# Expert rows turned by VectorE from quarter-wise row loads, with smaller rooms for three experts

## The chip, the cores and the metric

The kernel runs on one core of a Trainium2 chip. A core has TensorE (PE; PEld is its loading of weights), VectorE (DVE), ScalarE (ACT), GpSimd (POOL) and SyncE (SP), which issues most DMAs. Each engine works through its own queue in order, and semaphores join the queues. The metric is the device time of one execution in microseconds (us); smaller is better. The kernel before takes 770.73 us (median of three runs, 770.66 to 772.34).

## What is computed

```python
def _attn_ref(r, k, v, w, u) -> np.ndarray:
    B, H, S, D = r.shape
    state = np.zeros((B, H, D, D), dtype=np.float32)
    y = np.zeros_like(r)
    for t in range(S):
        kt, vt, rt = (k[:, :, t], v[:, :, t], r[:, :, t])
        cur = np.einsum('bhd,bhe->bhde', u[None] * kt, vt)
        y[:, :, t] = np.einsum('bhd,bhde->bhe', rt, state + cur)
        state = w[None, :, :, None] * state + np.einsum('bhd,bhe->bhde', kt, vt)
    return y.astype(np.float32)

def _moe_ref(x, w_in, w_out) -> np.ndarray:
    h = x @ w_in
    g = h - np.tanh(h)
    return (g @ w_out).astype(np.float32)

def _moe2_ref(x, expert_emb, tau, w1, w2) -> np.ndarray:
    N, D = x.shape
    E = expert_emb.shape[0]
    xn = x / (np.linalg.norm(x, axis=-1, keepdims=True) + 1e-06)
    en = expert_emb / (np.linalg.norm(expert_emb, axis=-1, keepdims=True) + 1e-06)
    logits = xn @ en.T / tau
    expert_idx = np.argmax(logits, axis=1)
    logits_shift = logits - logits.max(-1, keepdims=True)
    probs = np.exp(logits_shift)
    probs /= probs.sum(-1, keepdims=True) + 1e-09
    gate_w = probs[np.arange(N), expert_idx]
    out = np.zeros((N, D), dtype=np.float32)
    for e in range(E):
        mask = expert_idx == e
        if not mask.any():
            continue
        h = np.maximum(x[mask] @ w1[e], 0.0)
        out[mask] = gate_w[mask, None] * (h @ w2[e])
    return out.astype(np.float32)

def reference(**kwargs):
    moe_kwargs = {k[4:]: kwargs[k] for k in kwargs if k.startswith('moe_')}
    moe2_kwargs = {k[5:]: kwargs[k] for k in kwargs if k.startswith('moe2_')}
    attn_kwargs = {k: kwargs[k] for k in kwargs if not k.startswith(('moe_', 'moe2_'))}
    attn_out = _attn_ref(**attn_kwargs)
    B, H, S, D = attn_out.shape
    x = np.ascontiguousarray(attn_out.transpose(0, 2, 1, 3)).reshape(B * S, H * D)
    x = _moe_ref(x=x, **moe_kwargs)
    return _moe2_ref(x=x, **moe2_kwargs)
```

There are 3072 tokens of 384 columns. An attention with decay (4 batches, 8 heads of 48) is followed by a feed-forward layer of 2048 columns with x - tanh(x), and by eight experts of 1024 columns with relu, of which each token takes the one with the largest logit. All is float32. The rows per expert are, for these inputs, 430, 401, 394, 382, 379, 373, 368 and 345.

## The kernel before

All large products are made of three matmuls: each operand x is split into a rounded half `hi` and a rest `lo` = x - `hi`, and hi*hi, hi*lo and lo*hi are summed in one PSUM bank. ScalarE copies the rounded half, VectorE or POOL subtracts.

**Tanh stage.** Tokens go in blocks of 384 (three tiles of 128), j = 0 to 7, over 16 chunks of 128 FFN columns. `ffn1` (line 557) makes `ph`, `small_tanh` makes `ghi` (line 625) and `glo` (line 635), and `ffn2` (line 572) adds to three banks `acc`, some steps later, so that PE has other products meanwhile. In the first two blocks the weights are converted in between: `split` (line 276) is a ScalarE copy (line 277) and a POOL subtraction (line 278), and `Logits.turn` turns two chunks of w_out on PE (line 293) and copies them out (`wt`, line 295), for the eight columns by which the logits come out of the same product.

**Routing.** `finish` finds the expert and the place of each row of a block. The row is copied from `acc` to `xr` (line 673), or for block 0 added to `part`, and POOL scatters it to `xe` in DRAM, where each expert has a region; `tab` gets 16 integers a row, with token and gate. The experts are sorted by their number of rows. For the expert of rank i there is room for 384 + `MORE[i]` rows (ranks 0 to 2) or 384 - `LESS[i]` (the others); what doesn't fit goes to a slower loop at the end, `overflow`.

**Expert stage.** `rows` (line 840) loads an expert's rows from `xe`, by one SP DMA for each tile of 128 (line 846), into `xg` (which lies in the tiles named `rkv`) or, for the overflow tile, `xo` (`ktab`, `u_bc`). `columns` (line 902) turns each tile by three PE transposes of 128x128 into the bank `pt` (line 908), from which ScalarE takes `hi` (line 910) and VectorE `lo` (line 912, columns `xt`, `x5`, `xn`). `wide` makes the FFN of 8 chunks: nine `ffn1` matmuls of the room's width, `relu` (`ghi` line 651, `glo` line 653), and `ffn2` two chunks later. Then `put` scales the rows by the gate (`ob`, line 917) and scatters them to the output. `narrow_half` does the first expert's overflow tile with tokens and columns exchanged: line 1036, then `half_b`, `ghi5` (line 1056) and `accn`.

`load_expert` brings an expert's weights in four quarters `eraw` (lines 859, 862), through two buffers in turn, so quarter c + 2 can be loaded when quarter c is converted (`wq`, ScalarE line 885, VectorE line 886; POOL does half of expert 0's). The rows of expert jb + 1 are asked for when expert jb begins, and are turned at its chunk 6. Only expert 1's rows can't be: the last block's rows are scattered while expert 0 is at work.

**Order.** A tile framework's scheduler decides in what order the instructions of one engine stand, by its own cost estimates; `tc.issue_after(x)` keeps what it encloses from being placed ahead of x. PSUM has eight banks, which all tiles of tag `p` share in turn.

Of the kernel before, what the change touches and what calls it, by code (L numbers as in the profile page):

```python
# [29 lines left out]
def rwkv__then__tanh_ffn__then__top1_moe_kernel(  # L30
# [36 lines left out]
    MORE = (64, 64, 32)  # L67
    KOV = len(MORE)
    LESS = (0,) * (E - 2) + (16, 32)
# [212 lines left out]
    class Logits:  # L282
# [5 lines left out]
        def turn(self):  # L288
            self.wts = []
            for i in range(2):  # L290
# [4 lines left out]
                nc.scalar.activation(out=wt, in_=pt, func=AF.Copy)  # L295
# [268 lines left out]
    def ffn2(i, span, g, rhs, acc, ts=None):  # L564
        for t in ts or range(len(acc)):
            m = acc[t].shape[0]
            if t == TB:
                parts = [(g[0][:, TOK:TOK + m], 0), (g[0][:, TOK:TOK + m // 2], 1)][::-1 if i == span[1] - 1 else 1]
            else:
                parts = [(g[a][:, t * P:t * P + m], b) for a, b in ((0, 0), (0, 1), (1, 0))]  # L570
# [69 lines left out]
    def relu(ph, n, i):  # L640
        m = n - TOK
        if m <= 0:
            ghi = work.tile([P, TOK], F32R, name="ghi", bufs=LAG + 1)[:, :n]
            glo = work.tile([P, TOK], F32R, name="glo", bufs=LAG + 1)[:, :n]
        elif i % 2 == 0:
            ghi = work.tile([P, n + m], F32R, name="ghi4", tag="am", bufs=4)
            glo = work.tile([P, TOK], F32R, name="glo4", tag="am", bufs=4)
        else:
            g = work.tile([P, n + m + TOK], F32R, name="g4", tag="tt")
            ghi, glo = g[:, :n + m], g[:, n + m:]  # L650
        a = nc.scalar.activation(out=ghi[:, :n], in_=ph, func=AF.Relu)  # L651
# [276 lines left out]
    def wide(jb, sl):  # L928
# [20 lines left out]
        for i in range(NE):  # L949
# [24 lines left out]
        for t, (gt, g) in enumerate(sl):  # L974
# [687 lines left out]
```

## Time and profile before

| | |
|---|---|
| median of three runs | 770.73 us (770.66 to 772.34) |
| the profiled execution | 771.22 us |
| its span in the trace | 769.6 us, mean granted clock 0.995 |
| PE busy | 756.2 us (98%), 6143 instructions |
| DVE busy | 464.8 us (60%), 1037 |
| ACT busy | 457.1 us (59%), 1064 |
| POOL busy | 300.5 us (39%), 362 |
| expert rows' DMAs on SP (page part 6) | 22 of 192 KB in the group `rkv<-xe`, 4.4 us to landing |

The profile page gives, for one execution, each engine's busy time, the same in 40 slices of the span, the DMA queues, the chain of work that ended last, and the costliest groups of instructions. In the slices PE is at nine tenths or more except for the first and the last one and one near the start, in which the granted clock was lower. The engines' shares are averages over stages: attention and weight conversion lie in the first 200 us, the tanh stage goes on to about 540, and the experts fill the rest.

### The profile page before, as it was taken

The numbers are of one execution on the slowest core, as the hardware profiler recorded it, in microseconds if no ns is written. First come the engines' busy times: TensorE is split into PE (matmuls) and PEld (weight loads), VectorE is DVE, ScalarE is ACT, GpSimd is POOL, SyncE is SP. The second block draws the span as 40 slices with busy tenths as digits, with TensorE's granted clock in tenths as the row PEclk, the third lists the DMA queues.
The fourth block names the chain that finished last, engine by engine and source line by source line (L and its number), as shares of the span: only waits on it lengthen the run. The fifth ranks groups of instructions, "written<-read, shape, count | busy, mean of one in ns | idle before, by whom it ended". The sixth has DMA issues, their size and how long they took to land.

```text
span 769.6 us, 15995 instructions
## 1 busy us (share of the span) xinstructions
PE 756.2 (98%) x6143; PEld 718.4 (93%) x6143; DVE 464.8 (60%) x1037; ACT 457.1 (59%) x1064; POOL 300.5 (39%) x362
## 2 busy tenths in 40 slices
PE   9899999999999999999999999999999999999996
PEld 5689899999999999999999999999989999999996
DVE  7967976667656565565555655656684455545430
ACT  5787676655657556656657756768463535544431
POOL 3743680466781671753564341133530202110111
PEclk9899999999999999999999999999999999999999
DMA  8964355243240330232223101052374435454400
GB/s 263 288 206 142 118 170 200 64 165 100 66 148 24 126 122 2 91 94 87 80 69 123 59 32 64 14 171 85 116 229 143 129 115 189 150 173 161 154 31 32
DMA packets 41016, 92.21 MB, mean 120 GB/s; under 512 B 4827, under 2 KB 20597, under 8 KB 39907
## 3 DMA queue, kind: packets, MB, share of 16 engines
q1 hardware_dynamic: 36274, 81.44, 33.0%
q0 software_dynamic: 4240, 9.67, 3.5%
q8 instruction: 50, 0.82, 0.4%
q14 instruction: 36, 0.29, 0.1%
q10 hardware_dynamic: 416, 0.00, 0.0%
HBM read 67.26 MB, written 24.00 MB: 119 GB/s over the span
## 4 chain that ended last, share of the span: by engine, by line
PE 90%; issue 3%; DVE 3%; ACT 2%; DMA 2%; POOL 1%; POOLq 0%; SPq 0%; DVEq 0%; ACTq 0%
PE acc L572 39%; PE ph L557 37%; PE py L454 5%; PE pa L423 3%; DMA eraw<-in_moe_w_dram 2%; PE pt L908 1%; PE warm L158 1%; PE pst L475 1%; POOL out_dram L827 0%; PE pt L293 0%; DVE bits L267 0%; DVE wraw L270 0%; PE pl L303 0%; DVE bits L264 0%; PE accn L1036 0%
## 5 line engine op out<-in xcount | busy, mean ns | idle before, releaser
L557 PE MATMUL ph<-xt,wq 128*128 128x384 f32 (+4 forms) x1712 | 340.1, 341 | 1.9 <-ACT wt L295 1.3
L557 PEld LDWEIGHTS ph<-xt,wq 128*128 128x128 f32 x1712 | 302.7, 188 | 5.9 <-ACT wt L295 1.5
L572 PE MATMUL acc<-wq,ghi 128*128 128x392 f32 (+2 forms) x1120 | 289.1, 343 | 0.9 <-ACT ghi L625 0.9
L572 PEld LDWEIGHTS acc<-wq,ghi 128*128 128x128 f32 (+1 forms) x1120 | 200.3, 187 | 5.9 <-ACT ghi L625 1.2
L572 PE MATMUL acc<-wq,glo 128*128 128x392 f32 (+2 forms) x552 | 182.2, 340 | 0.1
L612 ACT ACTIVATE z<-ph 128x384 f32<-128x384 f32 x128 | 62.8, 490 | 105.0 <-PE ph L557 104.7
L623 DVE TENSOR_TENSOR ph<-ph,z 128x384 f32<-128x384 f32 x128 | 72.0, 563 | 62.6 <-ACT z L612 62.0
L572 PEld LDWEIGHTS acc<-wq,glo 128*128 128x128 f32 (+1 forms) x552 | 102.7, 187 | 0.9 <-DVE glo L635 0.7
L635 DVE TENSOR_TENSOR glo<-ph,ghi 128x384 fp32r<-128x384 f32 x128 | 70.7, 553 | 45.7 <-ACT ghi L625 45.6
L827 POOL DMA_INDIRECT out_dram<-ob,gts x27 | 27.2, 1008 | 176.6 <-ACT ob L917 171.4
L625 ACT ACTIVATE ghi<-ph 128x384 fp32r<-128x384 f32 x128 | 62.6, 490 | 41.0 <-DVE ph L624 37.6
L615 ACT ACTIVATE q<-z,sb_t 128x384 f32<-128x384 f32 x128 | 78.9, 617 | 3.4
L624 DVE SCALAR_TENSOR_TENSOR ph<-q,ph 128x384 f32<-128x384 f32 x128 | 71.7, 560 | 12.5 <-ACT q L615 3.5
L629 ACT ACTIVATE mk<-z,lz_t 128x384 bf16<-128x384 f32 x128 | 77.1, 603 | 0.0
L653 DVE SCALAR_TENSOR_TENSOR glo<-ph,ghi 128x384 fp32r<-128x384 f32 (+2 forms) x56 | 30.7, 549 | 63.8 <-ACT ghi L651 63.8
L651 ACT ACTIVATE ghi<-ph 128x384 fp32r<-128x384 f32 (+4 forms) x56 | 27.5, 491 | 67.6 <-PE ph L557 67.5
L411 POOL TENSOR_TENSOR am<-ident,cd 128x512 f32<-128x512 f32 x36 | 36.8, 1045 | 77.8 <-DVE cd L397 77.1
L886 DVE TENSOR_TENSOR wq<-eraw,wq 128x768 fp32r<-128x768 f32 x60 | 55.1, 955 | 11.5 <-ACT wq L885 11.0
L885 ACT ACTIVATE wq<-eraw 128x768 fp32r<-128x768 f32 x64 | 50.4, 839 | 6.2 <-DMA eraw<-in_moe_w_dram 6.2
L278 POOL TENSOR_TENSOR wq<-wraw,wq 128x768 fp32r<-128x768 f32 (+1 forms) x17 | 30.3, 1782 | 39.6 <-ACT wq L277 38.5
L716 POOL DMA_INDIRECT tab<-tk,irow x24 | 24.4, 1019 | 31.8 <-DVE tk L744 25.1
L491 POOL TENSOR_TENSOR st<-st,pw 112x384 f32<-112x384 f32 x20 | 16.7, 840 | 49.2 <-DVE st L484 43.7
(287 smaller groups left out, 860.0 us busy)
## 6 DMA issues: line engine op xcount, KB each, us to landing
eraw<-in_moe_w_dram SPq DMA_DIRECT2D x32, 768.0 KB, 4.5
rkv<-in_rows_dram SPq DMA_DIRECT2D x18, 640.0 KB, 5.6
tt<-in_cols_dram SPq DMA_DIRECT2D x22, 448.0 KB, 4.4
xd<-xt SPq DMA_DIRECT2D x8, 1152.0 KB, 8.0
wraw<-in_moe_w_in_dram SPq DMA_DIRECT2D x8, 768.0 KB, 8.6
wraw<-in_moe_w_out_dram SPq DMA_DIRECT2D x8, 768.0 KB, 5.2
rkv<-xe SPq DMA_DIRECT2D x22, 192.0 KB, 4.4
xe<-zero SPq DMA_DIRECT2D x2, 1536.0 KB, 15.4
```

What stands on the lines that cost most here:

```text
L454: nc.tensor.matmul(out=self.py[32 * g:32 * g + 32, kk, :], lhsT=lhs, rhs=rhs, start=start, stop=stop)
L557: mark["ph"] = nc.tensor.matmul(out=ph, lhsT=lhs[a][:, kk, :], rhs=rhs(b, kk), start=(kk == 0 and p == 0), stop=(kk == nk - 1 and p == 2)).ins
L572: mm = nc.tensor.matmul(out=acc[t][:lhs.shape[1]], lhsT=lhs, rhs=rhs(b, i), start=(i == span[0] and p == 0), stop=(i == span[1] - 1 and p ...
L612: nc.scalar.activation(out=z, in_=ph, func=AF.Square)
L615: nc.scalar.activation(out=q, in_=z, func=AF.Square, scale=SS, bias=sb_t)
L623: nc.vector.tensor_tensor(out=ph, in0=ph, in1=z, op=ALU.mult)
L624: nc.vector.scalar_tensor_tensor(out=ph, in0=q, scalar=KC, in1=ph, op0=ALU.add, op1=ALU.mult)
L625: mark["ghi"] = nc.scalar.activation(out=ghi, in_=ph, func=AF.Copy).ins
L629: nc.scalar.activation(out=mk, in_=z, func=AF.Relu, bias=lz_t, accum_out=zx[:, step:step + 1])
L635: mark["glo"] = nc.vector.tensor_tensor(out=glo, in0=ph, in1=ghi.bitcast(F32), op=ALU.subtract).ins
L885: nc.scalar.activation(out=hi[c][:, a], in_=t[:, a], func=AF.Copy)
L886: engs[s % len(engs)].tensor_tensor(out=lo[c][:, a], in0=t[:, a], in1=hi[c][:, a].bitcast(F32), op=ALU.subtract)
```

## The change

1. Rows are stored with another order of columns (`by_quarter`, `quarters`): the 384 columns are seen as 3 x 4 x 32 (k, j, c) and written as (j, k, c). So a quarter j of a row, 96 columns in one piece of 384 bytes, holds for each k the j-th 32 columns of it.
2. `rows` loads a tile by four DMAs on SP instead of one: DMA j puts quarter j of all 128 rows on partitions 32 j to 32 j + 31, with the row's block of 32 and the 96 columns along the free axis.
3. `columns` then turns the whole tile by one VectorE instruction, which transposes blocks of 32x32, into the PSUM bank `pt`. What follows reads `pt` as before. (`plain` serves only the overflow loop.)
4. `MORE` goes from (64, 64, 32) to (64, 32, 16) and `LESS` from (0, 0, 0, 16, 32) for ranks 3 to 7 to (0, 0, 8, 16, 32). `relu`, `ffn2`, `joined` and `wide` pad the second half of an overflow tile to a multiple of 32 rows, and `order_rest` has four more small operations.
5. Two placements: the split of the chunk that comes just before the fifth pair of logit columns is held back until after that pair's `wt` copies, and the steps i = 13 and 15 of the last tanh block place expert 0's weight loads behind `ghi`, where before only i = 15 did.

```diff
-    MORE = (64, 64, 32)
+    MORE = (64, 32, 16)
     KOV = len(MORE)
-    LESS = (0,) * (E - 2) + (16, 32)
+    SQ = 32
+    NQ = P // SQ
+    DQ = DM // NQ
+    LESS = (0,) * (E - 3) + (8, 16, 32)
...
-                nc.scalar.activation(out=wt, in_=pt, func=AF.Copy)
+                mark["wt"] = nc.scalar.activation(out=wt, in_=pt, func=AF.Copy).ins
...
-                parts = [(g[0][:, TOK:TOK + m], 0), (g[0][:, TOK:TOK + m // 2], 1)][::-1 if i == span[1] - 1 else 1]
+                parts = [(g[0][:, TOK:TOK + m], 0), (g[0][:, TOK:TOK + (m + 31) // 64 * 32], 1)]
+                parts = parts[::-1 if i == span[1] - 1 else 1]
...
+        h = (m + 31) // 32 * 32
         if m <= 0:
             ghi = work.tile([P, TOK], F32R, name="ghi", bufs=LAG + 1)[:, :n]
             glo = work.tile([P, TOK], F32R, name="glo", bufs=LAG + 1)[:, :n]
         elif i % 2 == 0:
-            ghi = work.tile([P, n + m], F32R, name="ghi4", tag="am", bufs=4)
+            ghi = work.tile([P, TOK + 2 * h], F32R, name="ghi4", tag="am", bufs=4)
             glo = work.tile([P, TOK], F32R, name="glo4", tag="am", bufs=4)
         else:
-            g = work.tile([P, n + m + TOK], F32R, name="g4", tag="tt")
-            ghi, glo = g[:, :n + m], g[:, n + m:]
+            g = work.tile([P, 2 * TOK + 2 * h], F32R, name="g4", tag="tt")
+            ghi, glo = g[:, :TOK + 2 * h], g[:, TOK + 2 * h:]
...
+    def quarters(x):
+        return x.rearrange("p (k j c) -> p j k c", k=NK, j=NQ)
+
+    def by_quarter(x):
+        return x.rearrange("p (j k c) -> p j k c", k=NK, j=NQ)
...
-                nc.vector.tensor_tensor(out=x, in0=acc[t], in1=x, op=ALU.add)
+                nc.vector.tensor_tensor(out=by_quarter(x[:, :DM]), in0=quarters(acc[t][:, :DM]), in1=by_quarter(x[:, :DM]),
+                                        op=ALU.add)
+                nc.vector.tensor_tensor(out=x[:, DM:], in0=acc[t][:, DM:], in1=x[:, DM:], op=ALU.add)
...
-                nc.scalar.activation(out=xr, in_=acc[t][:, :DM], func=AF.Copy)
+                nc.scalar.activation(out=by_quarter(xr), in_=quarters(acc[t][:, :DM]), func=AF.Copy)
...
-            g = (xg[(jb % 2) * TB + t] if t < TB else xo[jb % 2])[:m]
-            mark["rows"] = nc.sync.dma_start(out=g[:, :DM], in_=xe[bass.ds(row + t * P, m), :]).ins
+            n = (m + SQ - 1) // SQ
+            g = (xg[(jb % 2) * TB + t] if t < TB else xo[jb % 2])[:, :n * DQ]
+            src = xe[bass.ds(row + t * P, n * SQ), :].rearrange("(i r) (j e) -> j r i e", r=SQ, j=NQ)
+            for j in range(NQ):
+                mark["rows"] = nc.sync.dma_start(out=g[j * SQ:(j + 1) * SQ].rearrange("r (i e) -> r i e", i=n),
+                                                 in_=src[j]).ins
...
-    def columns(sl, hi, lo, gate):
-
-        for t, (_, g) in enumerate(sl):
-            m = g.shape[0]
-            pt = ps.tile([P, NK, m], F32, tag="p", name="pt")
-            for kk in range(NK):
-                nc.tensor.transpose(pt[:, kk, :], g[:, kk * P:(kk + 1) * P], ident[:m, :m])
+    def columns(sl, hi, lo, gate, plain=False):
+
+        for t, (gt, g) in enumerate(sl):
+            m = gt.shape[0]
+            n = (m + SQ - 1) // SQ
+            pt = ps.tile([P, NK, n * SQ], F32, tag="p", name="pt")
+            if plain:
+                x = work.tile([P, DM], F32, name="xp", tag="z")
+                nc.scalar.activation(out=quarters(x), in_=by_quarter(g), func=AF.Copy)
+                for kk in range(NK):
+                    nc.tensor.transpose(pt[:, kk, :], x[:, kk * P:(kk + 1) * P], ident)
+            else:
+                nc.vector.transpose(out=pt.rearrange("p k (i r) -> p i k r", r=SQ),
+                                    in_=g.rearrange("p (i k c) -> p i k c", i=n, k=NK))
+            pt = pt[:, :, :m]
...
-                    nc.scalar.activation(out=part[:, t, :], in_=x, func=AF.Copy)
+                    nc.scalar.activation(out=by_quarter(part[:, t, :DM]), in_=quarters(x[:, :DM]), func=AF.Copy)
+                    nc.scalar.activation(out=part[:, t, DM:], in_=x[:, DM:], func=AF.Copy)
...
+            with tc.issue_after(mark["wt"]):
+                while held:
+                    split(*held.pop())
...
-            last = split(*ready[m])
+            if turns.get(i + 1) == 4:
+                held.append(ready[m])
+            else:
+                last = split(*ready[m])
...
-                with tc.issue_after(mark["ghi"]) if i == 15 else ExitStack():
+                with tc.issue_after(mark["ghi"]) if i >= 13 else ExitStack():
```

The scheduler makes of it other orders on several engines. On ScalarE, in the second block of the tanh stage, some 82 us into the trace, the rows were these before; `wt` are the turned columns of w_out, `wq_80` is a converted weight chunk:

```order
L615 ACTIVATE q<-z,sb_t 128x384
L629 ACTIVATE mk,zx<-z,lz_t 128x384
L312 ACTIVATE wq_79<-pw__1257 128x2x8
L277 ACTIVATE wq_80<-wraw 128x2x384
L295 ACTIVATE wt<-pt 128x384 x2
L625 ACTIVATE ghi<-ph 128x384
L612 ACTIVATE z<-ph 128x384
L615 ACTIVATE q<-z,sb_t 128x384
```

and are now these:

```order
L616 ACTIVATE z<-ph 128x384
L619 ACTIVATE q<-z,sb_t 128x384
L633 ACTIVATE mk,zx<-z,lz_t 128x384
L315 ACTIVATE wq_79<-pw__1255 128x2x8
L298 ACTIVATE wt<-pt 128x384 x2
L280 ACTIVATE wq_80<-wraw 128x2x384
L629 ACTIVATE ghi<-ph 128x384
L616 ACTIVATE z<-ph 128x384
L619 ACTIVATE q<-z,sb_t 128x384
```

The pair of `wt` copies has passed the weight chunk's copy.

On ScalarE in the last tanh block, around 512 us, `wq_72` and `wq_73` are the first two quarters of expert 0's weights, and `ex` and `se` belong to the gates of the block before. Before:

```order
L625 ACTIVATE ghi<-ph 128x384
L885 ACTIVATE wq_72<-eraw 128x768 x2
L612 ACTIVATE z<-ph 128x384
L615 ACTIVATE q<-z,sb_t 128x384
L629 ACTIVATE mk,zx<-z,lz_t 128x384
L885 ACTIVATE wq_73<-eraw 128x768 x2
L625 ACTIVATE ghi<-ph 128x384
L736 ACTIVATE ex<-l 128x24
```

and now:

```order
L633 ACTIVATE mk,zx<-z,lz_t 128x384
L629 ACTIVATE ghi<-ph 128x384
L752 ACTIVATE ex<-l 128x24
L616 ACTIVATE z<-ph 128x384
L755 ACTIVATE se<-se,half 128x3
L619 ACTIVATE q<-z,sb_t 128x384
L633 ACTIVATE mk,zx<-z,lz_t 128x384
L905 ACTIVATE wq_72<-eraw 128x768 x2
L629 ACTIVATE ghi<-ph 128x384
L905 ACTIVATE wq_73<-eraw 128x768 x2
L616 ACTIVATE z<-ph 128x384
```

The conversions stood in front of the `z` after which `ex` comes; now they stand behind `ex`, `se` and the operations of one more chunk.

On VectorE where expert 0 passes to expert 1, around 555 us, `glo_7287` and `glo_7314` before are `glo_7315` and `glo_7342` now (chunks 5 and 6 of expert 0); `wq30_81` and `wq31_82` are the first two quarters of expert 1's weights, `xt` and `x5` its columns, and lines 1091 to 1107 before (1120 to 1136 now) belong to a list of what overflows. Before:

```order
L653 SCALAR_TENSOR_TENSOR glo_7287<-ph_7276,ghi_7286 128x384
L886 TENSOR_TENSOR wq30_81<-eraw_7018,wq20_78 128x768 x2
L653 SCALAR_TENSOR_TENSOR glo_7314<-ph_7303,ghi_7313 128x384
L886 TENSOR_TENSOR wq31_82<-eraw_7020,wq21_79 128x768
L1091 TENSOR_TENSOR g1_7583<-jot_7566,exc_7581 128x168
L886 TENSOR_TENSOR wq31_82<-eraw_7020,wq21_79 128x768
L912 TENSOR_TENSOR xn_7330<-pt_7331,xn_7330 128x3x64
L1093 TENSOR_TENSOR sel_7584<-g1_7583,sel_7584 128x168
L912 TENSOR_TENSOR xt_7337<-pt_7339,xt_7337 128x2x128
L912 TENSOR_TENSOR x5_7338<-pt_7339,xt_7337 128x128
L1099 SCALAR_TENSOR_TENSOR exc_7581<-exc_7581,reg_144 128x8
L912 TENSOR_TENSOR xt_7337<-pt_7346,xt_7337 128x2x128
```

and now, from the transpose of the second tile on:

```order
L934 STREAM_TRANSPOSE pt_7370<-rkv1_124 128x4x3x32
L662 SCALAR_TENSOR_TENSOR glo_7315<-ph_7304,ghi_7314 128x384
L1126 TENSOR_REDUCE oex_7621<-g1_7613 128x21
L906 TENSOR_TENSOR wq30_81<-eraw_7027,wq20_78 128x768 x2
L1131 TENSOR_TENSOR g1_7613<-exc_7611,jp_7615 128x168
L1136 CAST ovi_151<-oex_7621 128x21
L934 STREAM_TRANSPOSE pt_7375<-rkv1_124 128x4x3x32
L940 TENSOR_TENSOR xt_7363<-pt_7370,xt_7363 128x2x128
L940 TENSOR_TENSOR x5_7364<-pt_7370,xt_7363 128x128
L662 SCALAR_TENSOR_TENSOR glo_7342<-ph_7331,ghi_7341 128x384
L934 STREAM_TRANSPOSE pt_7380<-u_bc_139 128x96
L1132 TENSOR_TENSOR g1_7613<-g1_7613,sel_7614 128x168
```

The transposes and joins of the columns have come in between the two `glo` and the conversions, and the conversion of `wq31_82` comes next after the last row shown. On PE the products from the second `glo` now stand behind the first products of the narrow tile, just ahead of expert 1's first `ffn1`.

## Rows read from the trace of the kernel before

**Rows 1.** Busy us by stretch (PE, PEld, DVE, ACT, POOL; clock; DMA; GB/s):

```profile
540.00:570.00 30.00, 30.00 (x178) 28.18 (x178) 22.39 (x82) 15.24 (x33) 14.21 (x23) 1.00 0.53 151
645.00:670.00 25.00, 25.00 (x147) 24.96 (x147) 12.10 (x19) 11.25 (x21) 2.96 (x3) 1.00 0.49 158
```

**Rows 2.** Groups of line 908: busy us, mean ns of one, idle before:

```profile
L908 PE MATMUL pt<-ident,rkv 128*128 128x128 f32 (+2 forms) x72 | 9.1, 271 | 0.0
```

**Rows 3.** Timeline, PE, expert 0's first tile: start us, us, instruction, count:

```profile
526.77 1.14 PE L908 MATMUL pt<-ident,rkv 128*128 128x128 f32 x9
527.67 0.60 PE L572 MATMUL acc<-wq,ghi 128*128 128x392 f32 x2
```

**Rows 4.** Groups by shape, line 557: busy us, mean ns, idle before:

```profile
L557 PE MATMUL ph<-xt,wq 128*128 128x448 f32 x64 | 15.9, 369 | 0.0
L557 PE MATMUL ph<-xt,wq 128*128 128x352 f32 x72 | 12.6, 323 | 0.0
```

**Rows 5.** Timeline, ACT and PE, 81 to 83; in brackets idle before:

```profile
81.41 0.88 ACT L277 ACTIVATE wq<-wraw 128x768 fp32r<-128x768 f32 x1
82.19 0.85 ACT L295 ACTIVATE wt<-pt 128x384 f32<-128x384 f32 x2
82.71 1.86 PE L557 MATMUL ph<-xt,wq 128*128 128x384 f32 x9 [1.33 <-ACT wt L295]
```

**Rows 6.** Timeline, ACT and PE, 506 to 522:

```profile
511.80 1.58 ACT L885 ACTIVATE wq<-eraw 128x768 fp32r<-128x768 f32 x2 [5.11 <-DMA eraw<-in_moe_w_dram]
521.51 0.98 PE L572 MATMUL acc<-wq,ghi 128*128 128x392 f32 x4 [0.91 <-ACT ghi L625]
```

**Rows 7.** Timeline, SP's DMA issues, expert 1's rows, then expert 2's:

```profile
547.80 0.57 SPq L846 DMA_DIRECT2D ktab<-xe  x1
548.59 2.35 SPq L846 DMA_DIRECT2D rkv<-xe  x3
586.44 1.52 SPq L846 DMA_DIRECT2D rkv<-xe  x3
```

**Rows 8.** Line 846 alone: issue ns min/median/max, first and last start:

```profile
L846 SPq DMA_DIRECT2D rkv<-xe x24: 332/345/904, 502.6 to 700.3; - x24
```

**Rows 9.** DMA issues, 545:560, then 560:568: KB, us to landing:

```profile
rkv<-xe SPq DMA_DIRECT2D x3, 192.0 KB, 2.9
tab<-tk,irow POOLq DMA_INDIRECT x3, 2.4
...
rkv<-xe SPq DMA_DIRECT2D x3, 192.0 KB, 6.3
```

**Rows 10.** Tile eraw, 490 to 600:

```profile
DMA to landing us min/median/max: 4.4/4.8/6.0
```

**Rows 11.** Timeline, DVE, 551 to 561:

```profile
551.12 0.56 DVE L653 SCALAR_TENSOR_TENSOR glo<-ph,ghi 128x384 fp32r<-128x384 f32 x1 [0.30 <-ACT ghi L651]
555.08 1.83 DVE L886 TENSOR_TENSOR wq<-eraw,wq 128x768 fp32r<-128x768 f32 x2 [0.18 <-ACT wq L885]
560.74 0.42 DVE L912 TENSOR_TENSOR xt<-pt,xt 128x256 fp32r<-128x256 f32 x1
```

**Rows 12.** Timeline, ACT and PE, 565 to 574:

```profile
565.63 3.04 ACT L885 ACTIVATE wq<-eraw 128x768 fp32r<-128x768 f32 x4
570.69 1.53 ACT L917 ACTIVATE ob<-acc,gts 128x384 f32<-128x384 f32 x3 [0.33 <-PE acc L572]
572.09 0.67 ACT L1056 ACTIVATE ghi<-pt 128x256 fp32r<-128x256 f32 x2
573.85 1.57 PE L1036 MATMUL accn<-wq,ghi 128*128 128x384 f32 x8
```

**Rows 13.** Busy us by stretch (as rows 1), then PE's timeline:

```profile
30.00:32.00 2.00, 0.43 (x2) 0.43 (x3) 2.00 (x5) 2.00 (x8) 1.89 (x2) 0.72 1.05 392
32.00:34.00 2.00, 1.14 (x6) 0.73 (x5) 2.00 (x3) 2.00 (x8) 2.00 (x2) 0.50 1.03 394
...
35.73 2.79 PE L557 MATMUL ph<-xt,wq 128*128 128x384 f32 x9
```

More of the change, by code (lines that the diff above doesn't have):

```diff
@@ L645, in relu @@
         elif i % 2 == 0:
-            ghi = work.tile([P, n + m], F32R, name="ghi4", tag="am", bufs=4)
+            ghi = work.tile([P, TOK + 2 * h], F32R, name="ghi4", tag="am", bufs=4)
             glo = work.tile([P, TOK], F32R, name="glo4", tag="am", bufs=4)
         else:
-            g = work.tile([P, n + m + TOK], F32R, name="g4", tag="tt")
-            ghi, glo = g[:, :n + m], g[:, n + m:]
+            g = work.tile([P, 2 * TOK + 2 * h], F32R, name="g4", tag="tt")
+            ghi, glo = g[:, :TOK + 2 * h], g[:, TOK + 2 * h:]
         a = nc.scalar.activation(out=ghi[:, :n], in_=ph, func=AF.Relu)
         for o, c in ((glo, slice(0, min(n, TOK))), (ghi[:, n:], slice(TOK, n)))[:1 + (m > 0)]:
-            v = nc.vector.scalar_tensor_tensor(out=o, in0=ph[:, c], scalar=0.0, in1=ghi[:, c].bitcast(F32),
-                                               op0=ALU.max, op1=ALU.subtract)
+            a0, a1 = ph[:, c], ghi[:, c].bitcast(F32)
+            if c.start and h > m:
+                o = o[:, :2 * h - m].rearrange("p (a b) -> p a b", b=m)
+                a0, a1 = (x[:, None, :].to_broadcast([P, (2 * h - m) // m, m]) for x in (a0, a1))
+            v = nc.vector.scalar_tensor_tensor(out=o, in0=a0, scalar=0.0, in1=a1, op0=ALU.max, op1=ALU.subtract)
         return (ghi, glo), {"a": a.ins, "v": v.ins}
+    def quarters(x):
+        return x.rearrange("p (k j c) -> p j k c", k=NK, j=NQ)
+    def by_quarter(x):
+        return x.rearrange("p (j k c) -> p j k c", k=NK, j=NQ)
     def finish(j, acc, part=None):
@@ L920, in joined @@
     def joined(acc):
-        m = acc.shape[0] // 2
+        h = (acc.shape[0] + 31) // 64 * 32
+        m = acc.shape[0] - h
         b = work.tile([P, DM], F32, name="half_b", tag="z")[:m]
-        nc.scalar.activation(out=b, in_=acc[m:], func=AF.Copy)
+        nc.scalar.activation(out=b, in_=acc[h:], func=AF.Copy)
         nc.vector.tensor_tensor(out=b, in0=acc[:m], in1=b, op=ALU.add)
@@ L958, in wide @@
             if len(pend) > lag:
-                acc.extend(ps.tile([P, DM], F32, tag="p", name=f"acc{t}")[:g.shape[0] * (1 + (t == TB))]
-                           for t, (_, g) in enumerate(sl) if i == lag)
+                acc.extend(ps.tile([P, DM], F32, tag="p", name=f"acc{t}")[:g.shape[0] + (t == TB and (g.shape[0] + 31) // 32 * 32)]
+                           for t, (g, _) in enumerate(sl) if i == lag)
                 ffn2(*pend.pop(0))
@@ L973, in wide @@
         prev = None
-        for t, (gt, g) in enumerate(sl):
+        for t, (gt, _) in enumerate(sl):
             with tc.issue_after(prev) if prev and jb == E - 1 else ExitStack():
@@ L985, in narrow @@
         xt = [work.tile([P, NK, P], F32R, name="xn", tag="q"), work.tile([P, NK, P], F32R, name="xn", tag="t", bufs=1)]
-        columns([slot], xt[0], ((xt[1], 0, NK),), {})
+        columns([slot], xt[0], ((xt[1], 0, NK),), {}, True)
         yield
@@ L1171, in general @@
                 nc.vector.tensor_copy(out=gt[:, 1:2].bitcast(F32), in_=g[:, DM:DM + 1])
-                for _ in narrow(0, (gt, g), alone=True):
+                for _ in narrow(0, (gt, g[:, :DM]), alone=True):
                     pass
@@ L1182, in gate_row @@
         junk = work.tile([P, DM], F32, name="gjunk", tag="t", bufs=1)
-        nc.scalar.activation(out=row[:, :DM], in_=acc[:, :DM], func=AF.Copy)
+        nc.scalar.activation(out=by_quarter(row[:, :DM]), in_=quarters(acc[:, :DM]), func=AF.Copy)
         nc.scalar.activation(out=junk, in_=row[:, :DM], func=AF.Square, accum_out=rn)
@@ L1446, in rwkv__then__tanh_ffn__then__top1_moe_kernel @@
     at = (-1, -1) + CONV
+    held = []
     turns = {at[order.index(2 * c + 1)] + 1: c for c in range(NF // 2)}
@@ L1610, in rwkv__then__tanh_ffn__then__top1_moe_kernel @@
             nc.gpsimd.dma_start(out=xo[0][:, :DM], in_=xe[bass.ds(row, P), :])
-            for _ in narrow(0, (gt, xo[0])):
+            for _ in narrow(0, (gt, xo[0][:, :DM])):
                 pass
```

## The prediction

> **What bounds the kernel now.** I read the page's first two parts first, then the busy times by stretch, then PE's waits, then the single instructions where the diff bites. TensorE is busy for all of 540 to 570 and of 645 to 670, at full clock, while VectorE has 22.39 of 30 and 12.10 of 25 us and ScalarE about half [rows 1]. So a PE instruction that goes away is time saved, and work given to VectorE costs nothing unless something that PE wants comes late. Outside the expert stage PE waits rarely; two of these waits lie where the change moves operations [rows 5, 6].
>
> **Removed: the transposes on PE.** Line 908 stands for 72 transposes of the full tiles [rows 2]; nine more, three each, turn the three overflow tiles: 81, nine for each of eight experts and nine for the overflow. Nine in a row are not worth their summed 1.14 us, since they overlap: the next product starts 0.90 us after the first of them [rows 3]. 9 groups x 0.90 = **8.1 us**, all of it on PE, where nothing else hides it.
>
> **Removed: columns of the first product.** FFN1 of an expert has 72 matmuls (8 chunks x 9). 448 columns take 369 ns and 352 take 323 [rows 4], so 46 ns for 96 columns. Rooms shrink by 32 (rank 1), 16 (rank 2) and 8 (rank 5): 56 x 72 x 46/96 ns = **1.9 us**. The narrower overflow products keep their column count, so they give nothing.
>
> **Moved: the held split.** At 82.71 PE had stood 1.33 us for the second of two `wt` copies on ScalarE, which stood behind a `wq` copy of 0.88 [rows 5]. In the new order (first pair of order fences) the copy stands behind them: the two come 0.78 earlier (82.19 - 81.41), and PE finds its columns that much sooner. Gain 0.8, and not the whole 1.33, since what is left is the two copies themselves. The subtraction that follows the copy is POOL's, and starts 0.8 later; it feeds a weight half that is read some steps on. Nothing else is queued on POOL that PE awaits there.
>
> **Moved: conversions of expert 0.** ScalarE stood 5.11 us for the first weight quarter, until 511.80, and what was behind it was late until PE stood 0.91 us for `ghi` at 521.51 [rows 6]. In the new order (second pair of fences) the first two conversions come two steps later, and the third about three. Against that, 9 more row loads stand ahead of the first weight load on SP: at 0.58 us each (below) it lands 5.2 later, at 517.0. ScalarE, which stood ready at 506.69 (511.80 - 5.11), gets there two steps of 3.2 and some 2.5 of their operations later, about 515.6; it stands 1.4, converts two halves (1.58), and `ghi` is out at 519.1, while PE wanted it at 521.51 - 0.91 = 520.6. The wait goes: gain **0.9**. At 0.80 a load `ghi` comes at 521.1 and half of it stays; the bounds are 0 and 0.9.
>
> Gains: 8.1 + 1.9 + 0.8 + 0.9 = **11.7 us**.
>
> **Added: the transposes on VectorE.** 27 instructions of up to 128x384. The trace has none. Every elementwise VectorE operation of that size takes 0.56 us [rows 11], and I take 0.55; twice that if it makes two passes, and not less. In the steady expert stretch VectorE is idle 12.9 of 25 us [rows 1], and a `glo` is used two steps after its `ph`, so 3 to 4 x 0.55 in each expert (25 us) is hidden: 0. On this price the Trainium skill ("VectorE: DVE Perf Modes", section "The three transpose paths") has 311 ns for a 128x128 bf16 tile, into SBUF, in 32x32 blocks. An estimate from it is 0.93 us for 384 columns; with three such instructions on the chain below the sum would be about 1 us higher, 764. No run of before shows the instruction.
>
> **Added: row loads.** 27 become 108. Where expert 1 follows expert 0 it cannot be hidden, since its rows become readable only at 547.80, when the last scatter is in. There 5 loads are issued, which land 2.9 us later [rows 7, 9]; now there are 20 on the same queue. The pace: three in 1.52 us in the steady state, the single one 0.345 [rows 7, 8], so (1.52 - 0.345)/2 = 0.58 us. At the boundary the first steps are slower: 548.59 - 547.80 = 0.79, and the slowest issue is 0.904. I take 1.0 for the first and 0.58 for the rest, and 2.9 to land: load 12 is there at 547.80 + 1.0 + 11 x 0.58 + 2.9 = 558.1, load 20 at 562.7.
>
> VectorE works in order, and the new order (third pair) puts the transposes ahead of `glo` and the weight conversions. From load 12 on: transpose 0.55 (558.65), `glo` 0.56, a conversion pair 1.83, a transpose 0.55, join 0.42 + 0.28, `glo` 0.56, a short transpose 0.3, the second pair 1.9, and four list operations between them 1.15 (an estimate, below the 0.42 for 256 columns): **566.2**. Only then is the buffer of the quarter free that the last weight load needs; that takes 4.8 (median [rows 10]): 571.0. ScalarE converts it (3.04 for four, 1.52 for two), and behind it in its queue stand three `ob` (1.53), a `ghi` (0.55) and the two `ghi5` (0.67) [rows 12]: 575.3; half of VectorE's work on these, 0.4: 575.7. PE's product from `ghi5` (`accn`) started at 573.85 [rows 12]; without the 1.6 us of transposes just ahead of it and 0.28 of columns it would at 571.97. **Cost 575.7 - 571.97 = 3.7 us**, seen as three waits: small for `glo`, about 1.3 for expert 1's columns, about 2.2 for `ghi5`.
>
> Bounds: at 0.50 us per load 0.9 less, 2.8. At the 0.80 of the boundary's first step load 20 decides: its chain ends at 548.8 + 19 p + 2.9 + 0.3 + 0.3 + 1.9 = 554.2 + 19 p, 3.2 later than 566.2, and the cost is 6.9. Below 2.8 it goes only if the order of arrival leaves the first pair of conversions ahead of the transposes; then near 0.
>
> The other expert boundaries have their rows loaded a whole expert (25 us) ahead: 12 x 0.58 = 7 us of SP there, hidden; only the first weight load behind them starts later, by some 5 us, and that buffer's conversion has 10 us of room. The extra `part` operations (3 on ScalarE, 3 on VectorE) and four small ones in `order_rest` lie where neither engine is the bound: 0.
>
> **Sum.** 771.2 - 11.7 + 3.7 = 763.2 for the profiled execution. That one was 0.5 over the median of 770.73: **762.7 us**.
>
> **Rivals.** (a) *The boundary costs nothing*: the loads land early enough, or slack absorbs them. 771.2 - 11.7 - 0.5 = 759.0. Against it: VectorE is busy three quarters there.
> (b) *The loads are slow.* Loads that share the engines with weights landed in 6.3, not 2.9 [rows 9]: the chain ends 3.4 later, 766.1; at 0.80 a load as well, 769.3. I put it at 767. The smaller pieces speak for it: each row is now read in pieces of 384 bytes. The Trainium skill ("DMA: Bandwidth & Descriptors", Specifications) asks for at least 512 B per transfer for full rate, and describes read-modify-write below that; by that rule the loads land late. The trace neither confirms nor excludes it: a scatter of rows of 64 bytes landed in 2.4, as soon as a load of full ones [rows 9].
> (c) *The clock falls.* At 30 to 32 PE was busy 0.43 of 2 us, and the granted clock fell to half (1.2 of 2.4 GHz) for about 6.8 us; nine products then took 2.79 in place of 1.86 [rows 5, 13]. If the waits at the boundary do that, 6.8 x (1 - 1.86/2.79) = 2.3 more: 765. For it: my longest wait, 2.2, is as long as that stretch. Against it: after the 1.33 at 82.71 nine products took 1.86, at full clock.
> (d) *Slower than before.* SP needs over 1.05 us a load through all 20: the chain ends at 554.2 + 19 p, and from 574.2 on its cost passes the gain of 11.7. One issue took 0.904, to which some 0.24 (0.58 - 0.345) come before the next: 1.14, so the pace is not unheard of. At 1.2 the chain ends 10.8 later, the cost is 14.5, and the time 773.5. Against it: 24 issues have a median of 0.345 [rows 8].
> (e) *It does not do what it says*: a room is too small for its expert and the overflow loop runs, with four weight loads of 4.8 and products not overlapped: 30 us or more, 790. The inputs would have to have other counts than the rooms were cut for.
>
> **How the numbers follow.** Chances: my forecast with its neighbours (c included) 0.62, (a) 0.15, (b) 0.14, (d) 0.07, (e) 0.02. About 0.3% (2.3 us: 768.4 and 773.0) is what a measurement of this kernel can tell from no change. Faster by more: forecast, (a) and two thirds of (b), 0.86, less 0.02 for errors in the gains: 0.84. Within 0.3%: the rest of (b) and the lower half of (d): 0.09. Slower: the upper part of (d), (e), and a clock loss on top of (b): 0.07. Range: from (a) less 1 (the rest of the 1.33 at 82, and the same again elsewhere), 758, to where (b) is nearly through, 769.
>
> **What would show it.** No transposes on PE in the expert stage, and nine groups of 0.90 gone; FFN1 matmuls of 416, 400 and 376 columns; no wait at 82 and at 521. At the boundary 20 row loads 0.58 apart, VectorE with a transpose of 0.55 in front of `glo`, and PE waits of 1 to 3 us for expert 1's columns and for `ghi5`, nowhere else. Wrong if a VectorE transpose takes over 1.1 us, if loads are over 0.80 apart or land after 6 us, if PE waits at a later boundary, or if the granted clock falls after 545.

## The result

The changed kernel takes 762.26 us (median of four runs, 761.75 to 763.27), the kernel before 770.69 on the same chips (769.03 to 772.34): a ratio of 0.990, 95% interval 0.9885 to 0.9914, 8.4 us less. The forecast was 762.7 us, in 758 to 769. The profiled execution took 762.01 us with a span of 760.4, so 9.2 less than that of before.

### The profile after

Busy us, share and instructions of each engine: PE has 81 instructions less, VectorE 11.5 us more.

```profile
PE 745.0 (98%) x6062; PEld 709.1 (93%) x6062; DVE 476.3 (63%) x1071; ACT 456.5 (60%) x1067; POOL 300.7 (40%) x362
```

Where the 9.2 us come from is read by following the same product through both traces. PE's timeline of the kernel before (the product at 82.71 is in [rows 5]), at four more places:

```profile
143.17 1.74 PE L557 MATMUL ph<-xt,wq 128*128 128x384 f32 x9
...
344.66 1.75 PE L557 MATMUL ph<-xt,wq 128*128 128x384 f32 x9
...
518.85 1.39 PE L557 MATMUL ph<-xt,wq 128*128 128x384 f32 x7
...
732.87 1.79 PE L557 MATMUL ph<-xt,wq 128*128 128x368 f32 x9
```

The same `ffn1` products in the changed kernel:

```profile
80.90 1.85 PE L560 MATMUL ph<-xt,wq 128*128 128x384 f32 x9 [0.42 <-ACT wt L298]
...
142.65 1.74 PE L560 MATMUL ph<-xt,wq 128*128 128x384 f32 x9
...
344.85 1.75 PE L560 MATMUL ph<-xt,wq 128*128 128x384 f32 x9
...
518.79 1.39 PE L560 MATMUL ph<-xt,wq 128*128 128x384 f32 x7
...
723.91 1.67 PE L560 MATMUL ph<-xt,wq 128*128 128x368 f32 x9
```

The changed kernel is 1.81 ahead at 82, 0.52 at 143, 0.19 behind at 345 and level at 519. All that is left at the end, 8.96 at the last expert, is made behind 519, by the transposes, the rooms and the end of the wait at 521. What was won ahead of that was lost again: 1.3 at the attention scores near 123 (the lead falls from 1.80 to 0.52 between the `ffn1` products at 118.43 and 131.10), and 0.7 near 343, where PE stood still twice for some 0.35 us and the profile shows nothing that it waited for. The second of these stops, on PE's weight loads:

```profile
343.31 0.19 PEld L576 LDWEIGHTS acc<-wq,ghi 128*128 128x128 f32 x1 [0.36 <-issue]
```

The traces of six of the ten kernels below have no such stop.

The one of PE's waits that is new and not shown below (us in total, times, longest):

```profile
PE pk L708 <- DVE oh L703: 0.3, 1, 0.3
```

The wait for `ghi` at 521 is gone, the one for `wt` is down from 1.33 to 0.42 [rows 5, 6]. In their place stands one wait, of 2.75 us, for the copies `ghi5` where expert 0 passes to expert 1, and a short one for the routing counts.

The new VectorE instruction (busy us, mean ns of one, idle before), and the first product in its new widths:

```profile
L934 DVE STREAM_TRANSPOSE pt<-rkv 128x384 f32<-128x384 f32 (+1 forms) x24 | 12.7, 566 | 2.6 <-DMA rkv<-xe 2.6
```

```profile
L560 PE MATMUL ph<-xt,wq 128*128 128x416 f32 x64 | 14.9, 354 | 0.0
L560 PE MATMUL ph<-xt,wq 128*128 128x400 f32 x64 | 14.2, 346 | 0.0
L560 PE MATMUL ph<-xt,wq 128*128 128x376 f32 x72 | 13.7, 335 | 0.0
```

Before, 448 columns were 369 ns [rows 4], and the widths from which the other two come:

```profile
L557 PE MATMUL ph<-xt,wq 128*128 128x416 f32 x64 | 14.6, 352 | 0.0
L557 PE MATMUL ph<-xt,wq 128*128 128x384 f32 x1440 | 283.5, 341 | 1.9 <-ACT wt L295 1.3 <-ACT xt L459 0.6
```

The 20 row loads at the boundary, on SP (start, us, count), and the twelfth of them alone:

```profile
545.68 1.92 SPq L865 DMA_DIRECT2D ktab<-xe  x4
547.79 7.99 SPq L865 DMA_DIRECT2D rkv<-xe  x12
555.97 1.89 SPq L865 DMA_DIRECT2D u_bc<-xe  x4
...
553.33 0.32 SPq L865 DMA_DIRECT2D rkv<-xe  x1
```

VectorE there:

```profile
555.18 0.59 DVE L934 STREAM_TRANSPOSE pt<-rkv 128x384 f32<-128x384 f32 x1 [0.67 <-DMA rkv<-xe]
555.68 0.53 DVE L662 SCALAR_TENSOR_TENSOR glo<-ph,ghi 128x384 fp32r<-128x384 f32 x1
556.36 1.80 DVE L906 TENSOR_TENSOR wq<-eraw,wq 128x768 fp32r<-128x768 f32 x2
...
560.29 1.80 DVE L906 TENSOR_TENSOR wq<-eraw,wq 128x768 fp32r<-128x768 f32 x2
```

ScalarE there, and PE's product that waits:

```profile
567.91 1.58 ACT L905 ACTIVATE wq<-eraw 128x768 fp32r<-128x768 f32 x2 [1.77 <-DMA eraw<-in_moe_w_dram]
569.51 1.52 ACT L945 ACTIVATE ob<-acc,gts 128x384 f32<-128x384 f32 x3
570.92 0.53 ACT L656 ACTIVATE ghi<-ph 128x416 fp32r<-128x416 f32 x1
571.32 0.68 ACT L1085 ACTIVATE ghi<-pt 128x256 fp32r<-128x256 f32 x2
572.52 1.67 PE L1065 MATMUL accn<-wq,ghi 128*128 128x384 f32 x8 [2.75 <-DVE ghi L1086]
```

### The profile page after: what moved, and what is told of

The parts are those of the page before. It is cut to its first block, busy times and chain, and to the rows that moved or that the text cites. A ratio compares the mean times of both kernels' runs of the same rounds, so it can differ in the third digit from the quotient of the medians.

```text
span 760.4 us, 16122 instructions
## 1 busy us (share of the span) xinstructions
PE 745.0 (98%) x6062; PEld 709.1 (93%) x6062; DVE 476.3 (63%) x1071; ACT 456.5 (60%) x1067; POOL 300.7 (40%) x362
## 3 DMA queue, kind: packets, MB, share of 16 engines
q1 hardware_dynamic: 47058, 81.42, 33.5%
## 4 chain that ended last, share of the span: by engine, by line
PE 85%; issue 5%; DVE 4%; ACT 2%; DMA 2%; SPq 1%; POOL 1%; POOLq 0%; DVEq 0%; ACTq 0%
PE acc L576 37%; PE ph L560 36%; PE py L457 5%; PE pa L426 3%; SPq L865 1%; PE pst L478 1%; DMA eraw<-in_moe_w_dram 1%; POOL wq L906 0%; POOL out_dram L843 0%; PE pt L296 0%; DVE wraw L273 0%; DVE bits L270 0%; PE pl L306 0%; PE accn L1065 0%; DVE bits L267 0%
## 5 line engine op out<-in xcount | busy, mean ns | idle before, releaser
L560 PE MATMUL ph<-xt,wq 128*128 128x384 f32 (+5 forms) x1712 | 337.5, 340 | 1.0 <-ACT xt L462 0.6
L576 PE MATMUL acc<-wq,ghi 128*128 128x392 f32 (+3 forms) x1120 | 287.2, 343 | 0.1
L576 PEld LDWEIGHTS acc<-wq,ghi 128*128 128x128 f32 (+2 forms) x1120 | 200.1, 186 | 4.9 <-issue 1.0
L662 DVE SCALAR_TENSOR_TENSOR glo<-ph,ghi 128x384 fp32r<-128x384 f32 (+3 forms) x56 | 30.6, 547 | 56.3 <-ACT ghi L656 51.2
L656 ACT ACTIVATE ghi<-ph 128x384 fp32r<-128x384 f32 (+5 forms) x56 | 27.2, 486 | 56.9 <-PE ph L560 55.7
```

What stands on the lines that cost most here:

```text
L560: mark["ph"] = nc.tensor.matmul(out=ph, lhsT=lhs[a][:, kk, :], rhs=rhs(b, kk), start=(kk == 0 and p == 0), stop=(kk == nk - 1 and p == 2)).ins
L576: mm = nc.tensor.matmul(out=acc[t][:lhs.shape[1]], lhsT=lhs, rhs=rhs(b, i), start=(i == span[0] and p == 0), stop=(i == span[1] - 1 and p ...
```

## Experiments

Times are medians, ratios are against the kernel before on the same chip. The executions of one kernel lie up to 4 us apart, so differences of 1 us between kernels are read from the traces.

### The held split undone

```diff
-            if turns.get(i + 1) == 4:
-                held.append(ready[m])
-            else:
-                last = split(*ready[m])
+            last = split(*ready[m])
```

> The changed kernel without the held split: the weight chunk's copy stands in front of the wt copies again. My prediction gave the move 0.8 us; the trace of the changed kernel has PE's wait for wt down from 1.33 to 0.42. Theory: the move is worth 0.9, so 763.2 where the changed kernel has 762.3, and the wait of about 1.3 at 82 is back. Rival: the move sets off other orders (eight PE products of the attention scores near 121 us that no longer alternate between two banks, 1.1 us), which eat it: 762.3 or less, and the scores alternate again.

763.93 us (ratio 0.9908, 0.9892 to 0.9925), not to be told from 762.26 by the times. On PE the wait is back. The `ffn1` product ahead of it, the one that waits and one near 519:

```profile
78.77 1.84 PE L560 MATMUL ph<-xt,wq 128*128 128x384 f32 x9
83.67 1.85 PE L560 MATMUL ph<-xt,wq 128*128 128x384 f32 x9 [1.20 <-ACT wt L298]
...
521.50 1.75 PE L560 MATMUL ph<-xt,wq 128*128 128x384 f32 x9
```

In the changed kernel the second and the third start at 80.90 and 518.79 (above), the first here:

```profile
76.77 1.84 PE L560 MATMUL ph<-xt,wq 128*128 128x384 f32 x9
```

So the changed kernel is ahead of this one by 2.00, 2.77 and 2.71. The 2.00 are scatter, as the engines' instructions stand in the same order till there; the move takes 0.8 off the wait, and 0.7 of it is still there at 519. The rival fell: the scores near 121 stand apart here as well, and cost the same 1.3, so it is not this move alone that splits them, and they don't eat its gain.

### Only the last weight load of expert 0 behind `ghi`

```diff
-                with tc.issue_after(mark["ghi"]) if i >= 13 else ExitStack():
+                with tc.issue_after(mark["ghi"]) if i == 15 else ExitStack():
```

> The changed kernel with only the last of expert 0's weight loads (i = 15) behind ghi. Theory: the later conversions are worth the wait of 0.9 at 521 and the short stalls around it (0.4): 763.5, and PE waits 0.5 to 1 for ghi near 520. Rival: the wait was ended by the other order alone (rows loaded in quarters make the conversions late anyway): 762.3, no wait there.

763.14 us (0.9906, 0.9889 to 0.9923), and no wait at 520: the rival holds. With quarter-wise loads the conversions are late in ScalarE's order without the move. The trace shows something else: behind the wait for `ghi5` (here 1.80) the granted clock fell to 0.57 over 4 us, so half for some 3.4 of them. Busy us by stretch (columns as in [rows 1]), and PE's timeline:

```profile
572.00:576.00 4.00, 4.00 (x15) 3.42 (x14) 0.66 (x5) 0.00 (x0) 0.98 (x1) 0.57 0.92 254
...
571.34 2.00 PE L1065 MATMUL accn<-wq,ghi 128*128 128x384 f32 x8 [1.80 <-DVE ghi L1086]
573.23 2.77 PE L560 MATMUL ph<-xt,wq 128*128 128x416 f32 x7
```

Seven products took 2.77 us. In the changed kernel's own trace, after a longer wait, the clock stayed, and the same seven took 1.58:

```profile
572.00:576.00 4.00, 3.48 (x19) 3.13 (x20) 1.85 (x9) 0.40 (x1) 1.90 (x2) 1.00 0.74 214
...
574.07 1.58 PE L560 MATMUL ph<-xt,wq 128*128 128x416 f32 x7
```

The traces of the kernels with the held split undone and with the old rooms have the same fall of 3.4 us at that place.

### The same with single loads and PE transposes

Two kernels have rows in natural order, one load a tile and PE transposes, with the smaller rooms and the held split: one with the move of i = 13, one without.

```diff
     def quarters(x):
-        return x.rearrange("p (k j c) -> p j k c", k=NK, j=NQ)
+        return by_quarter(x)
...
+            if by_pe(jb, t):
+                mark["rows"] = nc.sync.dma_start(out=g, in_=xe[bass.ds(row + t * P, m), :]).ins
...
+                for kk in range(NK):
+                    nc.tensor.transpose(pt[:, kk, :m], g[:, kk * P:(kk + 1) * P], ident[:m, :m])
```

> The changed kernel with rows in their natural column order, one load a tile, and three PE transposes a tile, as before; smaller rooms and both moves kept. Theory: the transposes are worth 8.1 us of their own pitch and about 1 more by what they do to the product that follows, and the wait at expert 1 (2.9) goes: 762.3 + 9.1 - 2.9 = 768.5. Rival (the terms of the prediction): 8.1 - 3.7, 766.7. Second rival: the expert stage is bound by something else than PE and the transposes were hidden: 763 or less.

> Rows in natural order, one load a tile, PE transposes, smaller rooms, the held split kept, but only i = 15 behind ghi as before. Tells what ended PE's wait of 0.9 us at 521: with the quarter loads it stayed away without the move. Theory: with single loads the conversions come early again, wait for the weight load on ScalarE, and the wait is back: 0.9 to 1.3 more than with the move (767.5), 768.6, and PE waits for ghi near 520. Rival: the other new orders have ended it, and nothing changes: 767.5, no wait there.

With the move 767.46 us (0.9966, 0.9953 to 0.9979), without 768.69 (0.9983, 0.9973 to 0.9993). The first is 5.2 over the changed kernel, between the two sums, and its span, 766.0, is 5.6 over. The wait of 2.75 and that of 0.3 for the counts are not there, so the transposes cost 8.3 us by the times and 8.7 by the spans. The second has ScalarE's long wait and PE's wait for `ghi` back:

```profile
512.49 1.59 ACT L913 ACTIVATE wq<-eraw 128x768 fp32r<-128x768 f32 x2 [5.18 <-DMA eraw<-in_moe_w_dram]
521.96 0.98 PE L576 MATMUL acc<-wq,ghi 128*128 128x392 f32 x4 [0.66 <-ACT ghi L629]
```

So with single loads the move is what ends that wait; with the quarter loads it isn't needed.

### The old rooms

```diff
-    MORE = (64, 32, 16)
+    MORE = (64, 64, 32)
...
-    LESS = (0,) * (E - 3) + (8, 16, 32)
+    LESS = (0,) * (E - 2) + (16, 32)
```

> The changed kernel with the rooms of before, 64, 64, 32 more and 16, 32 less. Theory: 56 columns x 72 products x 46/96 ns = 1.9 us, all on PE: 764.2. Rival: the narrower products are partly hidden by waits or weight loads: 762.3 to 763.

763.87 us (0.9914, 0.99 to 0.9928): 1.6 more, as the theory has it, though the intervals overlap. The time alone doesn't show it: this trace has 3.4 us at half clock at the boundary, which that of the changed kernel hasn't. The mean times of the products by width, under the profile after, do.

### Expert 1's last quarter converted behind `ghi5`

```diff
                     t = load(c)
+            if jb == 1 and c == 3:
+                yield
+                gate = {"g": mark["ghi5"]}
             m = n // 2
...
```

The generator is taken up again after the narrow tile's copies `ghi5`, whose instruction is marked.

> The changed kernel, but ScalarE's conversion of expert 1's last weight quarter is placed behind the copies ghi5 of the narrow tile. Theory: what PE waits for at the boundary is only ScalarE's order, a weight load behind which ghi5 stands; the quarter itself is wanted some 15 us later. Then the wait of 2.8 us for ghi5 goes, 0 to 0.5 is left, and the time is 759.5. Rival: VectorE's chain (transposes, glo, conversions) is late by itself, the wait only changes its name, and the time stays at 762.

758.24 us (0.9849, 0.983 to 0.9867), the fastest kernel of this study. ScalarE's `ghi5` now stands ahead of the conversion, and PE's `accn` has no wait; the last row is the first product that reads the quarter, `ffn2` of expert 1's chunk 4:

```profile
567.98 0.68 ACT L1093 ACTIVATE ghi<-pt 128x256 fp32r<-128x256 f32 x2
568.50 1.62 ACT L908 ACTIVATE wq<-eraw 128x768 fp32r<-128x768 f32 x2
569.78 1.57 PE L1073 MATMUL accn<-wq,ghi 128*128 128x384 f32 x8
...
588.92 0.51 PE L576 MATMUL acc<-wq,ghi 128*128 128x384 f32 x2
```

That settles what PE waited for: not VectorE's chain, whose transposes and loads are unchanged, but a weight conversion ahead of `ghi5` in ScalarE's queue. Of the 4.0 us 2.75 are the wait as the trace of the changed kernel has it. In four other kernels with the same order on ScalarE there (the held split undone, i = 15 alone, the old rooms, and the scores below) PE waits 1.8, 1.8, 2.4 and 1.4 us for `ghi5`, and in the first three the clock falls behind it; here there is neither.

### The attention scores kept alternating

```diff
+                    with tc.issue_after(prev) if prev and chain else ExitStack():
-                    nc.tensor.matmul(out=self.pa[g][:, q, :], lhsT=self.KT[o:o + D, q, :], rhs=self.RT[o:o + D, q, :],
-                                     start=True, stop=True)
+                        prev = nc.tensor.matmul(out=self.pa[g][:, q, :], lhsT=self.KT[o:o + D, q, :],
+                                                rhs=self.RT[o:o + D, q, :], start=True, stop=True).ins
...
```

> The changed kernel with the order of the attention scores held to alternate between the two banks (rows 0 to 47 and 64 to 111 of TensorE). In the changed kernel one tile's 16 products near 121 us stand as 8 and 8, each 8 in 1.09 us, where 16 alternating take 1.09. Theory: the new order cost 1.1 us there, and one tile at 27 us that was never alternating 0.5: 760.7. Rival: the chip overlaps them by something else, or the next wait takes it: 762.3.

> Both orders mended in the changed kernel: expert 1's last weight quarter converted behind ghi5, and the attention scores held to alternate. Theory: the two are apart in time and add up; the landmarks put the scores at 1.4 us and the conversion at 3 to 4: 756.8. Rival: they don't add up since the scheduler moves something else for it: 758.2 as with the conversion alone.

What it mends, on PE before:

```profile
123.67 1.17 PE L423 MATMUL pa<-tt 48*128 48x128 f32 x16
```

and after the change:

```profile
121.34 1.16 PE L426 MATMUL pa<-tt 48*128 48x128 f32 x8
123.51 1.16 PE L426 MATMUL pa<-tt 48*128 48x128 f32 x8
```

Alone it took 760.30 us (0.9881, 0.9858 to 0.9904), together with the late conversion 758.55 (0.9848, 0.9834 to 0.9863), where the conversion alone had 758.24. The order does alternate in both (the first two products apart from the other 14), and at the place it brings 0.7: between the same two `ffn1` products lie 11.39 us in the kernel before (120.23 to 131.62), 12.67 after (118.43 to 131.10) and 11.99 with the order held (119.29 to 131.28). The medians of the sum don't show it; both traces have a wait of 0.8 to 0.9 for VectorE near 50 that the others lack, and the scatter is larger. The 2.0 us of the first result are mostly something else: its trace lacks the stop near 343, and PE waits half as long for `ghi5`, with ScalarE and VectorE in the same order there as in the changed kernel:

```profile
570.10 1.68 PE L1067 MATMUL accn<-wq,ghi 128*128 128x384 f32 x8 [1.44 <-DVE ghi L1088]
```

So the length of that wait scatters too.

### Every VectorE transpose twice

```diff
+                for _ in range(2):
                   nc.vector.transpose(out=pt.rearrange("p k (i r) -> p i k r", r=SQ),
```

> The changed kernel with every VectorE transpose done twice, into the same bank: 27 more of 0.27 to 0.58 us. Theory: only the three or four on the chain at the boundary cost, up to 2 us: 763.5 to 764.5, and no new wait at the later boundaries. Rival: VectorE is near its bound in the expert stage: up to 15 us more, 777.

762.08 us (0.9898, 0.9876 to 0.992): 27 more transposes cost nothing that the time shows. VectorE in a steady expert stretch, doubled and then as changed:

```profile
640.00:665.00 25.00, 25.00 (x144) 25.00 (x143) 15.67 (x25) 12.38 (x22) 2.97 (x3) 1.00 0.59 176
```

```profile
640.00:665.00 25.00, 25.00 (x144) 25.00 (x143) 14.13 (x23) 12.50 (x22) 2.97 (x3) 1.00 0.56 171
```

At the boundary PE has three waits of 0.55 to 0.78 in place of one of 2.75: the scheduler chose another order for this kernel.

### Twice as many loads at the boundary

```diff
+                h = SQ // 2 if jb == 1 or (jb, t) == (0, TB) else SQ
+                for r in range(0, SQ, h):
...
+                        in_=src[j][r:r + h]).ins
```

> The changed kernel with the 20 row loads at the boundary cut into 40 of half the rows. Theory: the queue takes 0.5 to 0.7 us a load whatever its size, the chain ends 10 to 13 us later, and so does PE's product from ghi5: 772 to 775, slower than before the change. That is the slower rival of the prediction, made. Rival: the pace follows the pieces (32 rows x 4 pieces each), half as long for half a load: 762.3.

772.27 us, slower than before (1.0032, 1.0019 to 1.0046): the theory, and the prediction's slower rival. The queue needs as long for a load of 16 rows as for one of 32. SP, PE's longest wait, and busy us by stretch:

```profile
545.43 5.23 SPq L867 DMA_DIRECT2D ktab<-xe  x8
550.85 12.46 SPq L867 DMA_DIRECT2D rkv<-xe  x24
563.51 4.58 SPq L867 DMA_DIRECT2D u_bc<-xe  x8
...
570.21 2.79 PE L560 MATMUL ph<-xt,wq 128*128 128x416 f32 x7 [5.67 <-ACT xt L941]
...
566.00:570.00 4.00, 0.00 (x0) 0.00 (x0) 0.92 (x3) 0.22 (x2) 0.00 (x0) 0.92 0.24 16
570.00:576.00 6.00, 5.79 (x17) 5.67 (x18) 2.71 (x5) 2.26 (x5) 0.00 (x0) 0.50 1.03 314
```

24 loads take 12.46 us. PE waits 5.67 for expert 1's columns, has nothing at all from 566 to 570, and then works at half clock: seven products in 2.79. A second wait, of 2.76 us for `half_b`, follows at 579.

## Why the prediction was right, and where its terms were off

The sum held (8.0 forecast, 8.4 measured) because its two large terms did, and PE's wait at the boundary is the one that the working ends in. That it came out so close is in part luck: the transposes gave 0.7 more and the boundary took 1.0 less than forecast, against 1.1 for the attention scores and 0.3 for the counts, which the prediction had at nothing. And one trace says less than its digits: up to the product at 77 the kernels above (without the two with held scores) have the same order on all engines, and their traces lie up to 2.8 us apart there. Half clock near 31 lasted 6.8 us in the trace of before [rows 13] and 3.4 in that of after, and it is one or the other among them.

- **Transposes, 8.1.** Right for what was counted, and 0.7 short. The nine take 0.90 to the next product, but the two products behind them take 0.60 [rows 3] where two others take 0.52 (those at 525.70 and 530.41): a product that follows transposes starts its successor later. With it a group is worth 0.98, nine of them 8.8; the kernel with PE transposes gave 8.3 to 8.7.
- **Columns, 1.9.** 369 to 354, 352 to 346 and 341 to 335 ns are 72 x 27 ns = 1.9; 341 is the mean over all stages, and from 570 on 384 columns take 339, so it is 1.8 to 1.9.
- **Held split, 0.8.** The wait fell by 0.9 where 0.8 was worked out, and 0.7 is still there at 519, as the kernel without the move shows. That the trace of after has no lead left there has other reasons. The prediction counted new orders only where it had looked for them. The scheduler also set apart the two banks' attention scores, and 16 products that took 1.17 now take 1.16 twice: 1.1 us that no term stands for. All kernels above have this except the two with held scores, also those without the held split, without the move of i = 13, with the old rooms and with single loads. The `part` rows written in two pieces, which the prediction put at 0, are in all of them; whether that edit sets it off was not tried. The stop of 0.7 near 343 is most likely chance, as six of the ten kernels above don't have it.
- **Conversions, 0.9.** The wait went with the order that the working names: the first conversion stands behind two more steps. But the move isn't what brings this order; the delayed loads alone do, and the move does it only without them. The first weight load landed earlier than worked out: ScalarE takes it at 515.49 in the trace of after, not at 517.0.
- **VectorE transposes, 0.55.** 0.57, and hidden away from the boundary, even doubled. The estimate of 0.93 from the Trainium skill's figure for bf16 ("VectorE: DVE Perf Modes", section "The three transpose paths") was the worse one. The Trainium skill ("Vector Engine (DVE) Microarchitecture Reference", section "The reshape front-end and per-opcode configuration") says that the transpose is pipelined to sustain one element per cycle per lane; the trace agrees in so far as 384 float32 columns take 0.57, about the 0.55 of an elementwise `glo` of that size.
- **The boundary, 3.7.** 2.75, one wait where three were forecast. PE was ready for `accn` 24.1 us behind the first load (569.77 - 545.68), where the working has 24.2, so the mis-sized part is the chain, 1.0 shorter than worked out, by links that went both ways. The pace was 0.58 in the sum and (557.54 - 545.68)/19 = 0.62 on the chip, so nearly right. The landing was too long: the twelfth load is issued at 553.33, and VectorE, which stood waiting for it, turns its tile at 555.18, 1.85 us and not 2.9; a load is now a quarter as large, which may be why. The two together make 0.8. VectorE's work from there to the end of the second conversion pair (562.09) is 6.9, not 8.1. The last weight quarter, however, came 5.8 later (567.91), not 4.8. So the columns were there in time for PE, and only the last link made it wait, the quarter that is converted ahead of `ghi5`. And 2.75 is the longest of five such waits, 1.4 to 2.75 in the traces of kernels with the same order on ScalarE there; the size of the term is known no better than that.
- **Rivals.** (b) fell: the loads landed sooner than the 2.9 of before, not later. They are also smaller, which by itself doesn't test the Trainium skill's rule on 512 B ("DMA: Bandwidth & Descriptors", Specifications). What the queue took in all says more (page part 3, q1): 81.44 MB in 36274 packets took 33.0% of the span before, 81.42 MB in 47058 packets 33.5% after, which is 254.0 and 254.7 us. So reading the rows in pieces of 384 bytes cost next to nothing, and nothing here bears out the rule. (c) is real, though not in the trace of after: three other kernels show the clock fall behind this wait, 3.4 us of it. (d) needs twice the loads to come true. (a) is what the late conversion shows to have been there to take.

## What to carry to other kernels

When work leaves the engine that bounds a kernel, follow the chain on the others to the one place where its input arrives last, and look there at what stands in an engine's queue ahead of what is waited for: here the new loads cost PE something only through a weight conversion that nobody needed for another 20 us, and with that moved the wait was gone. A change in one stage can move the order in another where a scheduler sets it; lay the same instructions of both traces side by side at a few places, and see where the lead is made and lost. And the price of these small loads was their place in the issuing queue, so cutting one into four costs four places.

## What was not expected of the hardware

- Products on rows 0 to 47 and on rows 64 to 111 of TensorE that write to two banks take 1.17 us for 16 when they alternate, and 1.16 for 8 when each half stands alone. The Trainium skill ("TensorEngine Tiling (Array Packing)", section "Key Properties") says that different tiles of the array can run in parallel; the trace shows it for neighbours in the queue, and not for the two halves with five other products between them.
- A load of 16 rows and one of 32 take the queue the same 0.52 us (12.46 for 24), and a load of 48 KB landed within 1.85 us of its issue where one of 192 KB had taken 2.9.
- At the same place PE's waits of 1.8, 1.8 and 2.4 us were followed by 3.4 us at half clock, in three traces, and waits of 1.4 and 2.75 by none, in two others.
